# Nystromformer attention with a feed-forward layer: batch 0's turn and first products in parts, x blocks in pair tiles, and the order of steps written out as a list

## The chip, the cores and the metric

The kernel runs on one core of a Trainium2 chip. The metric is the device time of one execution in microseconds; the time of a kernel is the median of its runs. A core has a matrix engine (TensorE, PE in the profile; PEld is its loading of weights), VectorE (DVE), ScalarE (ACT), GpSimd (POOL), and DMA queues, issued here by SyncE (SP). Each engine takes its own instructions in the order in which the program gives them, and engines wait for each other through semaphores.

## The reference

Inputs are q, k and v of [8 batches, 8 heads, 576 rows, 64], float32, gains g of 512, and two weight matrices, W1 of 512 x 2048 and W2 of 2048 x 512. For each batch and head:

```python
q_lm = q.reshape(B, H, 32, 18, D).mean(axis=3)     # 32 landmarks
k_lm = k.reshape(B, H, 32, 18, D).mean(axis=3)
A, Bm, C = sm(q, k_lm), sm(q_lm, k_lm), sm(q_lm, k)  # softmax(a b^T / 8)
Z = Bm.T / (norm1(Bm) * norminf(Bm) + 1e-06)
for _ in range(6):
    Z = 2 * Z - Z @ Bm @ Z
attn = A @ Z @ C @ v
x = attn as [8, 576, 512]                            # heads side by side
xn = (x - mean(x)) / sqrt(var(x) + 1e-06) * g
out = x + maximum(xn @ W1, 0) @ W2
```

## The kernel before, in words

**Tiling.** Products are in float16 with float32 sums in PSUM. Two heads share a tile (a "unit"); a batch has four of them (two tiles of four heads for the wide stages). The landmarks are sums over groups of 18 rows, made on PE (`sums`, batch 0) or on DVE. The softmaxes have no division where it can be put off: `ea` is exp of the scores of q against the key landmarks (A), `ec` that of k (C), and `st` holds Bm's product and the iterate side by side, so that one iteration (`iterate`, line 817) is eight small matmuls and one DVE instruction (2 st - psum). `gram_of` (797) makes the start of the iteration: a matmul with `bones` adds the columns, another makes the gram matrix; then DVE takes the maximum, a reciprocal and a product.

**Fewer steps than the reference.** C v, then Z of that, give `cv` and `zt`. The attention's rows x are needed only for the norm's statistics and the last sum; the first layer takes the product of A with `zt` W1 (`m16`, made by `First.products`, line 1440, from `w` and `zt`), and so works from ea (`psh <- ea, m`, four matmuls of 288 columns for each of the 16 chunks of 2048). W1 is scaled by the gains when it comes (`scale_w1`, 478, on POOL or ACT) and centred. For batch 0, which starts before W1's column means are known, a correction ("lesser", `less_mean`, 1393) stands in for it: four matmuls of 512 columns for each quarter of W1. The second layer runs 512 columns at a time over 16 chunks, from batch 4 on with some products of sums (`mix_ahead`, `seven_products`).

**Stages and order.** Batches run in sets (1), (2), (3,4), (5,6), (7) behind batch 0. Batch 0's attention is `attention0` (610): its order is written out, with yields between which the launch sequence (1916) puts loads and scalings. Before it, `turn_tile` (571) transposes each of four q and k tiles, nine blocks each, into `pst`, whose copy to `xT` ACT makes; the last tile's copy is one DVE copy of 1152 columns. `warm` (552) puts matmuls on a tile of zeros where PE would wait.

Everything later is given by five generators: attention, totals of landmarks, first layers, first rows, second layers. `run` (1888) asks at each turn a clock model (`Clock`, 85) which of them could go now and takes the first of them; `help_out` (1761) issues loads, casts, DVE jobs, statistics (`measure`), centring, and mixing between them, by when an engine is modelled to be free, and a table `AFTER` (1830) holds some steps back until others have been taken. The generated program is fixed before it runs; on the chip only the order within each engine and the semaphores are left.

**Rows.** For batches 5, 6 and 7 two blocks of 128 rows of x are made together (`two_rows`, 857): their products stand in PSUM by head parity, and four copies of 256 columns bring them into two tiles `xblk` of a pool of twelve (`xpool`), all four on the engine that is modelled to be free sooner (`sooner`, 604). All other blocks are made whole or in parts (`rows_of`, `part_of_rows`). `finish_block` takes the statistics, `second_layer` adds the product to the block in place, and `store` (1375) sends it out, after which its tile is free.

All instructions but matmuls (line 318), transposes on PE (322) and loads are issued through `keep`, so the profile puts them all on line 312. The W1 loads are line 475, the stores 1380.

Of the kernel before, what the change touches and what calls it, by code (L numbers as in the profile page):

```python
# [9 lines left out]
FP16 = mybir.dt.float16  # L10
# [10 lines left out]
def kernel(  # L21
# [26 lines left out]
    D2 = 2 * (D + 1)  # L48
# [24 lines left out]
    def keys_of(ap):  # L73
# [3 lines left out]
        at = [ap.offset]  # L77
# [7 lines left out]
    class Clock:  # L85
# [46 lines left out]
        def took(self, i, e, n, m):  # L132
# [3 lines left out]
            if e == "Pool":  # L136
# [4 lines left out]
                return 100 + 0.92 * n if "Copy" in op else 280 + 1.76 * n  # L141
            if n == 1152 and "Copy" in op:
                return 760
# [18 lines left out]
        def note(self, i):  # L162
# [26 lines left out]
            if type(i).__name__ == "InstDMACopy":  # L189
# [7 lines left out]
                late_ = 1500 if self.issued <= 5 else 600 + min(2200, 0.8 * (self.wire - start - 1650))  # L197
                done = self.wire + late_
                start = done
            elif e == "PE":  # L200
# [19 lines left out]
                else:  # L220
# [10 lines left out]
                    self.free[e] = start + (8 if rows_ == 64 and cols < 128 else 4)  # L231
# [15 lines left out]
            for n in reads:  # L247
                self.used[n] = max(self.used.get(n, (0.0, e)), (done, e))
                if n.startswith("m16") and ":" in n:
                    self.begun[n[:n.index(":")] + "."] = done  # L250
# [125 lines left out]
    zeros = const.tile([P, 256], FP16, name="zeros")  # L376
# [84 lines left out]
    xpool = Ring(name="xpool", bufs=12)  # L461
# [10 lines left out]
    def load_w1(i):  # L472
        f, half = divmod(i, 2)
        stg = stage.tile([P, 2, DM], FP32, name="wstg", tag="stg")
        keep(nc.sync.dma_start(out=stg[:], in_=w1_src[:, 2 * half:2 * half + 2, ts(f, DM)]))
# [81 lines left out]
    x_blk = {}  # L557
# [6 lines left out]
    nat_pss, early_xT = {}, {}  # L564
# [6 lines left out]
    def turn_tile(w, nm):  # L571
# [6 lines left out]
        last = (w, i) == (U - 1, 1)  # L578
        pst = ps2.tile([P, NJ, P], FP16, name="pst", tag="p2")
        if last:  # L580
            sums(w, i, n16)
        for j in range(NJ):
            TR(pst[:, j, :], n16[:, j, :, :].rearrange("p r d -> p (r d)"), ident16[:])
        if not last:
            scalar.copy(t[:], pst[:])
            sums(w, i, n16)
        return t, pst

    def divisors(ea):
# [5 lines left out]
        act(lns[:], lns[:], AF.Exp, scale=-1.0)  # L595
        return lns[:].rearrange("p a t -> p (a t)")

    def normalize(ea, engine):
        engine.tensor_tensor(out=ea, in0=ea, in1=divisors(ea), op=ALU.mult)
# [10 lines left out]
    def attention0():  # L610
# [18 lines left out]
        banks.release(*banks.held)  # L629
        dve.tensor_copy(out=last_tile[0][:], in_=last_tile[1][:])  # L630
        yield "landmarks"
# [8 lines left out]
        st, bmT = softmax_of(psb, W)  # L640
# [1343 lines left out]
```

## Time and profile before

| what | before |
|---|---|
| median of three runs | 263.51 us (263.14 to 263.57) |
| profiled execution, span | 261.4 us |
| around the span (median less span) | 2.1 us |
| PE busy | 252.8 us, 3519 matmuls |
| DVE, ACT, POOL busy | 209.9, 171.8, 136.8 us |
| DMA | 46.68 MB, 179 GB/s on the mean |

The profile is of one execution. "Busy" is the time in which an engine ran an instruction; idle time of an engine other than the bound costs nothing by itself. In the rows of the time line a line gives start, length, engine, source line, operation, output and inputs, and count; in brackets stands the idle time before it and the engine and tile that ended it. Matmuls overlap, so of two rows the difference of their starts is read, and not the length.

### The profile page before, as it was taken

The page shows a single profiled execution, that of the slowest core. Times are in us where ns is not written, and L with a number is a line of the kernel's source. Part 1 is how long each engine was busy: PE and PEld are TensorE (multiplying, and loading weights), DVE is VectorE, ACT ScalarE, POOL GpSimd, SP SyncE. Part 2 cuts the span into 40 slices and gives each one's busy share as a digit, 9 for nine tenths or more (in the row PEclk, how much of TensorE's full clock was granted, in tenths as well). Part 3 has the DMA queues.
Part 4 walks back from the last instruction along what each step waited for, and adds up shares of the span by engine and source line. Part 5 has one row for each costly group of instructions (what it writes and reads, how often), then busy time and mean ns, then how long its engine had stood idle before and what let it go on. Part 6 is the DMA issues. An engine that isn't in the chain of part 4 may idle for free.

```text
span 261.4 us, 8559 instructions
## 1 busy us (share of the span) xinstructions
PE 252.8 (97%) x3519; PEld 167.7 (64%) x3519; DVE 209.9 (80%) x480; ACT 171.8 (66%) x332; POOL 136.8 (52%) x162
## 2 busy tenths in 40 slices
PE   7899999999999999999999999999999999999994
PEld 6645754556455574546655466588878875888883
DVE  2767965999979997899996972999399889696862
ACT  2588986458956878489986669634977863766000
POOL 5288779999951889899899955400000014000000
PEclk9999999999999999999999999999999999999999
DMA  6999999999947998669731101110330007100705
GB/s 238 381 393 381 384 391 387 355 251 345 349 145 213 282 375 308 185 158 336 244 84 43 26 21 40 45 38 3 80 84 4 3 11 162 32 3 0 163 19 182
DMA packets 24142, 46.68 MB, mean 179 GB/s; under 512 B 2980, under 2 KB 3240, under 8 KB 24104
## 3 DMA queue, kind: packets, MB, share of 16 engines
q1 hardware_dynamic: 23624, 45.50, 54.5%
q10 hardware_dynamic: 480, 0.66, 0.7%
q8 instruction: 27, 0.44, 0.7%
q14 instruction: 11, 0.09, 0.1%
HBM read 36.70 MB, written 9.44 MB: 177 GB/s over the span
## 4 chain that ended last, share of the span: by engine, by line
PE 82%; DVE 11%; DMA 3%; ACT 2%; issue 1%; SPq 0%; DVEq 0%
PE bank L318 53%; PE psh L318 21%; DMA stg<-in_q_dram 3%; DVE m L312 2%; PE psd L318 2%; PE pscv L318 2%; DVE six L312 1%; DVE xblk L312 1%; DVE w L312 1%; DVE part L312 1%; ACT hT L312 1%; PE psea L318 1%; DVE nat L312 1%; DVE xT L312 1%; PE psec L318 1%
## 5 line engine op out<-in xcount | busy, mean ns | idle before, releaser
L318 PE MATMUL bank<-w,hT 128*128 128x512 f16 (+3 forms) x528 | 109.5, 335 | 0.0
L312 ACT ACTIVATE hT<-psh 128x576 f16<-128x576 f32 x123 | 76.7, 655 | 23.9 <-PE psh L318 22.2
L318 PE MATMUL psh<-ea,m 128*128 128x288 f16 x512 | 79.0, 286 | 0.4 <-DVE ea L312 0.3
L318 PEld LDWEIGHTS <-hT 128*128 128x128 f16 x656 | 60.3, 98 | 29.5 <-issue 4.7
L318 PEld LDWEIGHTS <-m 128*128 128x128 f16 x512 | 49.4, 98 | 19.3 <-issue 2.8
L312 DVE SCALAR_TENSOR_TENSOR xblk<-bank,rstd,xblk 128x256 f32<-128x256 f32 (+2 forms) x77 | 39.2, 543 | 14.8 <-PE bank L318 14.6
L312 POOL TENSOR_TENSOR ea<-ea,lns 128x576 f16<-128x576 f16 x14 | 18.2, 1318 | 53.1 <-ACT lns L312 51.8
L312 POOL CAST nat<-stg 128x1152 f16<-128x1152 f32 x23 | 26.1, 1147 | 11.3 <-DVE xT L312 8.7
L312 DVE BATCH_NORM_STATS2 six<-xblk 128x6 f32<-128x512 f32 x36 | 24.3, 674 | 0.6 <-ACT xblk L312 0.5
L312 POOL CAST natv<-stg 128x1152 f16<-128x1152 f32 (+1 forms) x17 | 19.4, 1166 | 9.4 <-DMA stg<-in_v_dram 7.9
L312 DVE STREAM_TRANSPOSE xT<-nat 128x576 uint32<-128x576 uint32 x28 | 21.2, 759 | 0.0
L318 PE MATMUL bank<-w2mix,hT 128*128 128x256 f16 x128 | 17.7, 273 | 0.0
L318 PE MATMUL bank<-w2mix 128*128 128x256 f16 x128 | 17.4, 273 | 0.0
L312 DVE SCALAR_TENSOR_TENSOR st<-st,bank 128x128 f16<-128x128 f16 (+3 forms) x36 | 13.2, 366 | 5.0 <-PE bank L318 4.8
L312 ACT ACTIVATE lns<-psd 128x576 f32<-128x576 f32 x16 | 10.3, 645 | 7.9 <-PE psd L318 7.7
L312 DVE TENSOR_REDUCE part<-xT 128x32 f16<-128x576 f16 x20 | 14.3, 744 | 0.1
L312 ACT COPY xblk<-bank 128x512 f32<-128x512 f32 (+1 forms) x19 | 11.0, 592 | 4.9 <-PE bank L318 4.8
L312 POOL TENSOR_TENSOR asum<-asum 128x256 f32<-128x256 f32 (+1 forms) x20 | 13.0, 650 | 1.6
L318 PEld LDWEIGHTS <-w2mix 128*128 128x128 f16 x128 | 12.3, 98 | 2.0
L312 ACT ACTIVATE ec<-psec 128x256 f16<-128x256 f32 (+1 forms) x42 | 12.0, 430 | 1.9 <-PE psec L318 1.8
L318 PEld LDWEIGHTS <-st 32*32 32x32 f16 (+1 forms) x380 | 6.5, 90 | 10.5 <-DVE st L312 6.3
L312 POOL TENSOR_TENSOR asum<-nat 128x512 f32<-128x512 f16 x10 | 11.7, 1172 | 1.1 <-ACT nat L312 0.4
(133 smaller groups left out, 375.2 us busy)
## 6 DMA issues: line engine op xcount, KB each, us to landing
stg<-in_q_dram SPq DMA_DIRECT2D x16, 576.0 KB, 6.7
stg<-in_k_dram SPq DMA_DIRECT2D x15, 576.0 KB, 6.0
out_dram<-xblk SPq DMA_DIRECT2D x66, 128.0 KB, 2.4
wstg<-in_moe_w_ch_dram SPq DMA_DIRECT2D x16, 512.0 KB, 7.2
stg<-in_v_dram SPq DMA_DIRECT2D x5, 576.0 KB, 7.7
stg<-in_v_dram SPq DMA_DIRECT2D x40, 72.0 KB, 2.8
stg<-in_v_dram SPq DMA_DIRECT2D x6, 288.0 KB, 5.7
stg<-in_v_dram SPq DMA_DIRECT2D x12, 144.0 KB, 3.1
```

The source lines that it names most:

```text
L312: return lambda *args, **kw: keep(getattr(self.engine, op)(*args, **kw))
L318: keep(nc.tensor.matmul(o, l, r, start=start, stop=stop, tile_position=(rb, cb), skip_group_check=(skip or cb != 0)))
```

## The change

Instructions of all kinds stay what they compute; the parts are:

1. **Pair tiles.** `x_of` gives two neighbouring blocks one tile [128, 2, 512] from a pool of 5; the last block of an uneven batch (block 4 of each nine) has a tile of its own from a pool of 2. `two_rows` makes 2 copies of 512 columns in place of 4 of 256, and each goes to the engine that is modelled to be free sooner: 6 on DVE and 6 on ACT, where there had been 20 and 4.
2. **Batch 0's last turn.** The last k tile is cast in two halves as before, with another pattern; of its nine transposes six stand ahead of the landmark products and three behind the first q scores; four go to `pst` and five to a bank, and two DVE copies (512, 640 columns) replace one of 1152.
3. **Batch 0's order.** Scores and iterations are interleaved otherwise: landmark product, q scores of the first tile, the three transposes, k scores, q scores of the second tile, then the gram, in a bank of its own and with no filler in between; the k scores of the second tile stand behind the first iteration; the turn of the gains (`scaled_by_pe`) stands behind the gram. `ea` of the first tile is scaled whole by POOL, that of the second in halves by DVE as before. The copies to `zt` go from ACT to DVE. The first products `m16` are copied in parts of 128, 128 and 256 columns (before 256, 256). The correction of W1's second quarter stands behind the first two chunks of the first layer and not ahead of them, those of the third and fourth a chunk later.
4. **W1's first quarter** is loaded by four DMAs of 256 KB, before two of 512 KB. POOL scales four pieces of it, then `ea`, then nine more.
5. **The filler** at the start is 11 matmuls of 384 columns and three times two of 384, before 27 of 160, three times three of 256, and six in the gram and products: 25 matmuls fewer.
6. **The list.** `help_out`, `AFTER` and the choice by the clock model are gone; `ORDER` names 12 kinds of step and is issued as it stands. A step that cannot be issued yet is kept and tried again after each following one. Stores and the norm's deviations are still issued by the clock model (`settle`).

On the engines: PE 3494 matmuls (3519), DVE 468 instructions (482), ACT 340 (340), POOL 170 (167). Two changes of the shape of PE tiles fewer (131, before 133).

The core of the diff:

```diff
-    xpool = Ring(name="xpool", bufs=12)
+    xpool = Ring(name="xpool", bufs=5)
...
-            x_blk[j] = xpool.pin(xpool.tile([P, DM], FP32, name="xblk", tag="xblk"))
+            if j % 9 == 4:
+                t = xpool.pin(xpool.tile([P, 1, DM], FP32, name="xblk", tag="xone", bufs=2))
+            else:
+                t = xpool.pin(xpool.tile([P, 2, DM], FP32, name="xblk", tag="xblk"))
...
-            copy = sooner(1024, clock.at(t))
-            for i, (j, _) in enumerate(mine):
-                for hp in range(2):
-                    copy(crossed(x_of(j), hp), to[:, hp, i, :, :].rearrange("p u (r d) -> p u r d", r=2))
+            for hp in range(2):
+                sooner(512, clock.at(t))(
+                    crossed(x, hp), to[:, hp, :, :, :].rearrange("p i u (r d) -> p i u r d", r=2))
...
-            for r in (range(2) if (nm, u) == ("k", U - 1) else (slice(0, 2),)):
-                dve.tensor_copy(out=t[:, :, r, :] if isinstance(r, int) else t[:].rearrange("p j r d -> p r j d"),
-                                in_=raw[nm, u][:, r, :, :])
+            for r in range(2) if (nm, u) == ("k", U - 1) else (None,):
+                if r is None:
+                    dve.tensor_copy(out=t[:].rearrange("p j r d -> p r j d"), in_=raw[nm, u][:])
+                else:
+                    dve.tensor_copy(out=t[:, :, r, :].rearrange("p j (a d) -> p a j d", a=2),
+                                    in_=raw[nm, u][:, r, :, :].rearrange("p j (a d) -> p a j d", a=2))
...
+        if f == 0:
+            parted[stg.name] = DM
+            for c in range(2):
+                keep(nc.sync.dma_start(out=stg[:, c, :], in_=w1_src[:, 2 * half + c, ts(f, DM)]))
...
+        turn(range(NBEFORE))
+        last_turn.extend((t, pst, rest, turn))
...
-        dve.tensor_copy(out=last_tile[0][:], in_=last_tile[1][:])
-        yield "landmarks"
+        t, pst, rest, turn = last_turn
+        dve.tensor_copy(out=t[:, 0:NFIRST, :], in_=pst[:, 0:NFIRST, :])
...
-        for w in range(W):
-            scores_of_q(w)
+        scores_of_q(0)
+        turn(range(NBEFORE, NJ))
+        scores_of_k(0)
+        scores_of_q(1)
+        st, bmT = softmax_of(psb, W)
+        dve.tensor_copy(out=t[:, NFIRST:NJ, :], in_=rest)
+        banks.release(*last_bank)
+        lns = []
+        _, csum = gram_of(p1([P, 4, W * LM], "psse"), st, bmT, W, None, p1([P, 4, W * LM], "gram"))
+        lns.append(divisors(ea[0], 0))
+        scaled_by_pe()
...
-            scalar.copy(zt[:, :, w, :], pszt[:, :, 0:LM])
-        copy_mean(0)
-        scale_w1(3, 1, scalar)
...
+        normalize_by(pool, ea[0], lns[0])
...
+        for w in range(W):
+            dve.tensor_copy(out=zt[:, :, w, :], in_=pszt[w][:, :, 0:LM])
...
-        less_mean(1)
         next(a0)
...
-            if m in (2, 5):
-                f = 2 if m == 2 else 3
+            if m in (1, 3, 6):
+                f = (m + 3) // 3
...
+    ORDER = (
+        "2 3 4 215 3 23 M 2 J2 3 22 J3 2 1 3 2 M 22 L J 0 J 2 J 12 L 2 1 2 42 3 M 0 4 0 L 3 2 "
...
+        for k in order + [None] * 400:
+            settle()
+            late = [x for x in late if not issue(x)]
...
+            elif k in late or not issue(k):
+                late.append(k)
...
-    warm(27, 160)
+    warm(11, 384)
...
-            warm(3, 256)
+            warm(2, 384)
```

In `ORDER` a digit or letter is a kind of step and the number behind it how many of them: 0 attention, 1 totals, 2 first layers, 3 first rows, 4 second layers, J a DVE job of the batches to come, M statistics, C centring of W1, X and W mixing, K a cast, L a load.

More of the change, by code (lines that the diff above doesn't have):

```diff
@@ L47 @@
     UP = 16.0
-    D2 = 2 * (D + 1)
+    D1, D2 = D + 1, 2 * (D + 1)
     scale_qk = 1.0 / (D ** 0.5)
@@ L1929 @@
         load_w1(i)
+        if i < 2:
+            for c in range(2):
+                scale_w1(i, c, pool)
+    for it in range(7):
+        next(a0)
+    for i in range(2, 8):
         for c in range(2):
-            if i % 2 == 0 or c == 0 or i == 1:
+            if i % 2 == 0 or c == 0:
                 scale_w1(i, c, pool)
@@ L1948 @@
             b1.next_cast(part={"V": None, "A": 0, "B": 1}[what])
-    for it in range(6):
-        next(a0)
-    next(a0)
     run()
-    help_out(True)
+    settle(True)
 _INS = ['q', 'k', 'v', 'moe_g_ln', 'moe_w_ch1', 'moe_w_ch2']
```

375 lines of the change are left out of this document (191 added, 184 removed), and 30 rows, old and new, of tables (AFTER, ORDER).

## The prediction

> **What bounds the kernel now.** I read the page first: busy time by engine, the slices, the chain that ended last.
>
> ```profile
> span 261.4 us, 8559 instructions
> ...
> PE 252.8 (97%) x3519; PEld 167.7 (64%) x3519; DVE 209.9 (80%) x480; ACT 171.8 (66%) x332; POOL 136.8 (52%) x162
> ...
> PE   7899999999999999999999999999999999999994
> ...
> GB/s 238 381 393 381 384 391 387 355 251 345 349 145 213 282 375 308 185 158 336 244 84 43 26 21 40 45 38 3 80 84 4 3 11 162 32 3 0 163 19 182
> ...
> PE 82%; DVE 11%; DMA 3%; ACT 2%; issue 1%; SPq 0%; DVEq 0%
> ```
>
> The matrix engine is the bound: 97% busy, 82% of the last chain. So only two things can shorten the run: matmul time that is removed, and time in which PE waits. The DMA works at some 385 GB/s in slices 2 to 7 (6.5 us each), so what is wanted early cannot simply come earlier. The table of windows says where PE is not full:
>
> ```profile
> 0.00:22.00 22.00, 18.03 (x319) 12.43 (x320) 13.21 (x41) 11.88 (x18) 13.15 (x38) 1.00 0.94 342
> 22.00:66.00 44.00, 43.40 (x514) 25.52 (x511) 36.95 (x84) 33.12 (x66) 39.07 (x41) 1.00 1.02 354
> ```
>
> Columns: window, its sum, then busy us and count of PE, PEld, DVE, ACT, POOL, the clock, the DMA share, GB/s. In the first 22 us 3.97 us of PE are empty, and part of its 18.03 is filler on zeros; in the next 44 only 0.6. The two places to price are therefore the start (batch 0's chain through DVE and ACT) and a few short stalls behind it. The span is 261.4 us, the median of the runs 263.51, so 2.1 us lie around the span; I add the change to the median.
>
> **The change part by part.**
>
> *Batch 0's chain.* PE, DVE and ACT rows of the start (start, length, engine, operation, count, idle before):
>
> ```profile
> 10.71 0.44 PE L318 MATMUL bank<-pm,nat 128*128 128x64 f16 x9 [0.21 <-DVE nat L312]
> 10.98 0.67 PE L322 MATMUL pst<-ident,nat 128*128 128x128 f16 x9
> ...
> 11.73 0.22 PE L318 MATMUL bank<-lm 64*32 64x32 f16 x8
> ...
> 13.15 0.19 PE L318 MATMUL bank<-st,bones 128*128 128x64 f16 x1
> ...
> 13.67 0.93 PE L318 MATMUL psa<-xT,lm 64*32 64x512 f16 x16
> 14.54 0.24 PE L318 MATMUL bank<-st 32*32 32x64 f16 x8
> ```
>
> ```profile
> 11.18 0.29 DVE L312 CAST lm<-bank 128x128 f16<-128x128 f32 x1 [0.20 <-PE bank L318]
> 11.68 0.76 DVE L312 COPY xT<-pst 128x1152 f16<-128x1152 f16 x1 [0.21 <-PE pst L322]
> 12.43 0.22 DVE L312 TENSOR_REDUCE rsum<-bank 128x2 f32<-128x64 f32 x1
> ```
>
> ```profile
> 12.94 1.19 ACT L312 ACTIVATE ect<-psc 128x576 f16<-128x576 f32 x2 [0.72 <-PE psc L318]
> ```
>
> ```profile
> L312 DVE CAST nat<-stg 128x1152 f16<-128x1152 f32 x3 | 2.3, 760 | 5.2 <-DMA stg<-in_q_dram 4.5 <-DMA stg<-in_k_dram 0.7
> L312 DVE CAST nat<-stg 128x576 f16<-128x576 f32 x2 | 1.5, 754 | 0.0
> ```
>
> Cast: PE waits at 10.71 for the second half of the last k. A half costs 754 ns, a whole tile of twice the elements 760. The change gives the halves another pattern. Bounds: 380 ns (half of 760) to 754 (no change); I take 450, nearer the whole tile's rate. Gain 0.30, sums from about 10.41. [...]
>
> Transposes: six instead of nine (some 0.07 each) and no gains' turn stand before the products at 11.73. They then wait for the landmarks' cast (11.18, 0.29), with the cast's gain at about 10.88 to 11.17, so they start near 11.22, 0.5 earlier. The three transposes left follow on PE behind the first q scores, where PE waits anyway. The row sum at 12.43 was behind the 0.76 copy; the copy of 512 columns is at most 0.38 by the same row's rate, and the sum follows ACT at about 11.76. Next late is ACT: the second q scores stand ahead of the bones matmul and need the buffer that the first exponential frees, 0.6 long (ACT's two of 1.19) and starting at about 11.75 behind that of the products (11.22, 0.22 on PE, and an estimated 0.3 for the small exponential, as the casts and sums of 64 or 128 columns take 0.22 to 0.29); bones goes from 13.15 to about 12.8. From there the gram had stood behind filler in one bank with the column sum; the gap from 13.15 to the first iteration's 14.54 shrinks from 1.39 to about 1.05, and the 0.93 us of q scores no longer lie in it. First iteration about 13.85, 0.7 earlier. The six iterations are a chain from PE to DVE and back, whose instructions the change leaves as they are, so their step stays.
>
> The rest of the chain:
>
> ```profile
> 19.07 0.52 PE L318 MATMUL bank<-w,zt 64*32 64x512 f16 x8 [0.25 <-ACT zt L312]
> 19.67 1.18 PE L318 MATMUL bank<-w,lesser 128*128 128x512 f16 x4
> 20.69 0.41 PE L318 MATMUL psh<-ea,m 128*128 128x288 f16 x2
> 21.38 1.14 PE L318 MATMUL psh<-ea,m 128*128 128x288 f16 x6 [0.28 <-DVE ea L312]
> ```
>
> ```profile
> L312 DVE TENSOR_TENSOR ea<-ea,lns x4: 444/450/818, 18.3 to 21.2; 128x288 f16<-128x288 f16 x4
> ```
>
> ```profile
> L312 POOL TENSOR_TENSOR ea<-ea,lns 128x576 f16<-128x576 f16 x14 | 18.2, 1318 | 53.1 <-ACT lns L312 51.8 <-PE pszc L318 1.3
> ```
>
> ```profile
> 16.25 6.60 POOL L312 TENSOR_SCALAR w<-wstg,g_sb 128x512 f16<-128x512 f32 x8 [0.28 <-DMA wstg<-in_moe_w_ch_dram]
> ```
>
> Behind the iterations the first products with W1 come about 0.6 earlier (18.45; DVE, which now makes both copies of zt in front of them, is assumed to lose 0.1 on ACT). Then PE ran 4 matmuls of the second quarter's correction ("lesser"), started the first chunk and waited 0.28 on DVE, which has four halves of ea to scale (shortest, median and longest in the tile's row). Two of them go to POOL as one instruction; the second chunk, of which the 21.38 group holds four (its start 21.87 by 122 ns a matmul), can start at about 20.62, 1.25 earlier. But the four lesser matmuls (4 x 0.216 = 0.86) that had lain in this wait now come behind the two chunks, on PE's full stretch. Net **-0.4**. Bounds: +0.4 (ea late, the 0.86 paid, 0.46 gained) and -1.0.
>
> POOL's ea must be in time: 1.32 us on POOL (the form's mean in later batches) between the scalings of W1 at 0.825 us each. It postpones the nine scalings behind it by 1.3 us; the second quarter is wanted only with the correction that now comes later, so I price that at nothing; if that cover goes, it costs up to 1.3. W1's four loads of 256 KB move the same bytes through SP's queue, two issues more; nothing, as the wire is the limit (385 GB/s), and the first half of a quarter can only land earlier.
>
> *Stalls of the body.* Where PE waits behind 22 us, and what the written list puts there:
>
> ```profile
> 34.46 1.00 PE L318 MATMUL psec<-xT,lm 32*32 32x288 f16 x32
> 35.73 0.19 PE L318 MATMUL bank<-st,bones 128*128 128x64 f16 x1 [0.27 <-DVE st L312]
> ...
> 40.74 0.24 PE L318 MATMUL bank<-st 32*32 32x64 f16 x8 [0.25 <-DVE st L312]
> ...
> 66.25 0.67 PE L318 MATMUL psec<-xT,lm 32*32 32x288 f16 x28
> 66.86 2.55 PE L318 MATMUL bank<-w,hT 128*128 128x512 f16 x11
> 69.24 0.19 PE L318 MATMUL bank<-st,bones 128*128 128x64 f16 x1
> 69.61 0.28 PE L318 MATMUL bank<-st 128*128 128x128 f16 x2 [0.17 <-DVE st L312]
> ...
> 76.20 0.59 PE L318 MATMUL bank<-w,hT 128*128 128x512 f16 x2
> 76.94 0.31 PE L318 MATMUL bank<-st 128*128 128x160 f16 x2 [0.15 <-DVE st L312]
> ```
>
> ```profile
> 39.60 0.69 DVE L312 BATCH_NORM_STATS2 six<-xblk 128x6 f32<-128x512 f32 x1 [0.53 <-ACT xblk L312]
> 40.43 0.25 DVE L312 SCALAR_TENSOR_TENSOR st<-st,bank 128x128 f16<-128x128 f16 x1
> ```
>
> A matmul of 512 columns takes 0.216 (66.86 to 69.24 for 11). Batch 1: psec to bones lasted 1.27, where 28 of the 32 took 0.61 at 66.25; about 0.6 is empty, and two matmuls of 512 (0.43) are put there: -0.4. Its first step at 40.74: the 0.69 of statistics stood ahead of the step's DVE instruction at 40.43; the list puts them behind: -0.3. Batch 2: bones ends at about 69.27, the next starts at 69.61 on DVE's st; 13 instead of 11 matmuls stand between: -0.34. Its step before 76.94: 0.74 for two matmuls of 0.216, 0.31 empty; the spacing is made more even: -0.2. Together -1.25. The list is issued without regard to the time, so elsewhere it can make new ones: I allow +0.4. Body: **-0.85**.
>
> *Tile form.* Two changes of form fewer on PE (131 against 133 by the order of both kernels).
>
> ```profile
> 44.22 0.60 PE L318 MATMUL bank<-w,hT 128*128 128x512 f16 x2
> ...
> 44.91 0.60 PE L318 MATMUL bank<-w,hT 128*128 128x512 f16 x2
> ```
>
> From 44.22 to 44.91 are 0.69, of which 0.43 are two matmuls: into small tiles and out costs 0.26 with the small matmuls between. Bounds 0 to 0.26; **-0.2**.
>
> *Pair tiles.* For batches 5 to 7:
>
> ```profile
> L312 DVE COPY xblk<-psr 128x256 f32<-128x256 f32 x20 | 7.1, 417 | 0.0
> ```
>
> Four copies of 256 columns (20 on DVE, 4 on ACT in all) become two of 512, six on each. One of 512 costs between one and two of 256, 0.42 to 0.83, so DVE loses 3.3 to 5.8 us of its 8.3 and ACT gains at most 3.3. Both engines have room and PE does not wait here, so **0**. If the cover goes: a pair holds two blocks until both are stored, and a wait for a pair tile delays one group of row matmuls, a few tenths.
>
> Sum: -0.4 - 0.85 - 0.2 = -1.45; 263.51 - 1.45 = **262.1 us**.
>
> **The rivals.**
> *R1, the start's gain is swallowed.* Batch 1's attention waits for its loads (the wire is full to 52 us), so an earlier start only shifts the wait. For it: slices 2 to 7. Against: PE has first-layer work of batch 0 to fill with. Also the case that the halved cast does not get faster. -1.05: 262.5.
> *R2, slower: the written list has no time check.* A DVE instruction of 0.69 ahead of an iteration's st step (as at 39.60) costs PE up to that. There are some 30 such steps. They take the place of the 0.4 allowed, so 1.85 of gains stand against them: three hits (2.07) are the point from which it is slower at all, four give 2.76 - 1.85 = +0.9, 264.4, five 265.1. For it: nothing holds a step back any more. Against: the places that I followed in the new order are spaced as the old ones or better.
> *R3, DVE slowed by POOL.* With ea on POOL, DVE's remaining halves run beside it. One of the four took 0.82 instead of 0.45, so both may: +0.74, -0.71 in all, 262.8. Against: POOL was busy from 16.25 without a break, and only one of four halves was slow. [...]
> *R4, more.* The correction's matmuls fall into other waits (a full -1.25) and no new stall appears: -1.25 - 1.25 - 0.2 = -2.7, 260.8.
>
> **How the numbers follow.** Forecast 0.40, R1 0.12, R3 0.08, R4 0.10, all faster than 263.51 by over 0.2% (0.53 us, about what a measurement of this kernel can tell from no change). R2 with two or three hits (263.0 to 263.7), within it: 0.12. R2 with more: 0.18. So 0.70, 0.12, 0.18. The range reaches from 260.2 (R4, with 0.6 more by the start's bound of -1.0) to 264.6 (R2 with four hits); it leaves out R2 with five or more, 0.1, and as little below.
>
> **What would show it.** In the changed kernel: the second half of the last k cast at 0.45 and not 0.75; first iteration at about 13.85; first W1 products at 18.45; second chunk at about 20.6 with four lesser matmuls behind it; the gaps before 35.7, 40.7, 69.6 and 76.9 gone; DVE's copies of rows shorter by 3.3 us or more. It would be wrong if PE showed new waits of 0.3 or more on DVE's st in the iterations of batches 1 to 7, or if PE waited for ea past 21.

## The result, and the profile after

The changed kernel takes 264.95 us (median of 6 runs, 264.48 to 266.12), the kernel before 263.32 (6 runs, three of them those of the table above). The ratio is 1.0061, interval 1.0042 to 1.0081: **slower by 0.6%, where 0.55% faster had been forecast**. The profiled execution has a span of 262.8 us (before 261.4). Medians here and below are of all runs, and the ratios leave out the few runs that took over 1.5% more than the fastest of their kernel.

The page of the changed kernel, first the lines that answer to those of before:

```profile
span 262.8 us, 8511 instructions
...
PE 253.7 (97%) x3494; PEld 166.5 (63%) x3494; DVE 204.4 (78%) x466; ACT 174.0 (66%) x332; POOL 139.7 (53%) x165
...
PE   7879999999999999999999999999999999999994
...
PEclk9986999999999999999999999999999999999999
...
GB/s 250 353 398 385 386 387 361 368 231 296 359 208 202 159 324 356 175 180 190 374 192 41 23 42 42 42 40 2 36 128 2 4 3 159 42 2 0 159 23 180
...
PE 83%; ACT 5%; POOL 3%; DVE 3%; DMA 3%; issue 2%; SPq 0%; ACTq 0%; POOLq 0%; DVEq 0%
```

PE does 25 matmuls less and is busy 0.9 us longer. The line to see is PEclk, the clock that PE was granted: 8 and 6 in slices 3 and 4 now, where the page of before has

```profile
PEclk9999999999999999999999999999999999999999
```

In the table of windows of the changed kernel (columns as in the prediction; the one before the DMA's share is the clock) this is a step:

```profile
15.00:16.00 1.00, 0.95 (x34) 0.46 (x26) 0.55 (x2) 1.00 (x3) 1.00 (x2) 1.00 1.07 406
16.00:17.00 1.00, 0.57 (x23) 0.32 (x20) 0.30 (x2) 0.97 (x3) 1.00 (x3) 1.00 1.02 387
17.00:18.00 1.00, 0.18 (x9) 0.17 (x8) 0.00 (x0) 0.33 (x1) 1.00 (x1) 0.79 1.06 399
18.00:19.00 1.00, 1.00 (x19) 0.32 (x14) 0.62 (x4) 0.00 (x0) 1.00 (x3) 0.50 1.04 383
...
23.00:24.00 1.00, 1.00 (x6) 0.61 (x5) 1.00 (x4) 0.65 (x1) 0.82 (x2) 0.50 1.05 393
24.00:25.00 1.00, 1.00 (x5) 0.45 (x4) 0.65 (x2) 0.73 (x2) 1.00 (x3) 0.79 1.00 349
```

From 17.59 to 24.41 us PE runs at half its clock. Ahead of it PE stands still, and the time line of PE says on what:

```profile
16.07 0.24 PE L322 MATMUL bank<-st 32*32 32x64 f16 x8
16.24 0.37 PE L322 MATMUL pscv<-natv,ect 64*64 64x130 f16 x11
17.82 0.48 PE L322 MATMUL pscv<-natv,ect 64*64 64x130 f16 x9 [1.22 <-issue]
...
20.94 0.63 PE L322 MATMUL bank<-w,zt 64*32 64x512 f16 x8
22.11 2.12 PE L322 MATMUL psh<-ea,m 128*128 128x288 f16 x8 [0.54 <-DVE m L316]
24.03 1.23 PE L322 MATMUL bank<-w,lesser 128*128 128x512 f16 x4
```

The wait of 1.22 us lies in the middle of twenty matmuls with the same inputs, and "issue" means that PE waited for nothing that the profile shows. In the kernel before the same stretch has no wait:

```profile
15.83 0.24 PE L318 MATMUL bank<-st 32*32 32x64 f16 x8
15.99 0.49 PE L318 MATMUL bank<-natv,ect 64*64 64x130 f16 x20
```

The eight matmuls at 22.11 take 0.24 us each (to 24.03), twice the 0.122 of before (eight from 29.88 to 30.86).

Where the time goes is seen best when both kernels are read at the same amount of matmul work: columns times the form of a matmul over 128*128, the largest form in the rows, filler left out. As the orders of the two differ, a figure is good to about 0.2 us. Microseconds by which the changed kernel is behind the one before:

```
time in the kernel before  15.4   17.6   19.9   23.1   33.8   46.2   99.1   250
changed                   -0.4   +1.5   +2.6   +2.5   +2.9   +2.4   +1.6   +1.3
```

It is ahead at 15.4, loses 3.0 us between 15.4 and 20, and wins back 1.3 by the end.

### The profile page after: what moved, and what is told of

The parts are those of the page before. It is cut to its first block, busy times and chain, and to the rows that moved or that the text cites. A ratio compares the mean times of both kernels' runs of the same rounds, so it can differ in the third digit from the quotient of the medians.

```text
span 262.8 us, 8511 instructions
## 1 busy us (share of the span) xinstructions
PE 253.7 (97%) x3494; PEld 166.5 (63%) x3494; DVE 204.4 (78%) x466; ACT 174.0 (66%) x332; POOL 139.7 (53%) x165
## 4 chain that ended last, share of the span: by engine, by line
PE 83%; ACT 5%; POOL 3%; DVE 3%; DMA 3%; issue 2%; SPq 0%; ACTq 0%; POOLq 0%; DVEq 0%
PE bank L322 53%; PE psh L322 23%; DMA stg<-in_q_dram 3%; POOL asum L316 2%; PE pscv L322 2%; ACT hT L316 1%; PE psec L322 1%; POOL ea L316 1%; PE psea L322 1%; ACT xblk L316 1%; PE psd L322 1%; ACT m L316 1%; PE psr L322 1%; ACT ea L316 1%; DVE st L316 0%
## 5 line engine op out<-in xcount | busy, mean ns | idle before, releaser
L322 PE MATMUL bank<-w,hT 128*128 128x512 f16 (+3 forms) x528 | 111.1, 334 | 0.0
L316 ACT ACTIVATE hT<-psh 128x576 f16<-128x576 f32 x126 | 79.2, 654 | 19.1 <-PE psh L322 17.8
L322 PE MATMUL psh<-ea,m 128*128 128x288 f16 x512 | 80.6, 288 | 0.7 <-DVE m L316 0.5
L316 POOL TENSOR_TENSOR ea<-ea,lns 128x576 f16<-128x576 f16 x15 | 19.5, 1314 | 49.3 <-ACT lns L316 49.3
L316 POOL CAST nat<-stg 128x1152 f16<-128x1152 f32 x25 | 28.9, 1172 | 11.5 <-DVE xT L316 7.9
L316 POOL CAST natv<-stg 128x1152 f16<-128x1152 f32 (+1 forms) x17 | 19.3, 1163 | 12.5 <-DMA stg<-in_v_dram 8.7
L316 ACT CAST m<-bank 128x512 f16<-128x512 f32 x17 | 9.8, 591 | 6.0 <-PE bank L322 5.2
```

Source lines behind the costliest of these rows:

```text
L316: return lambda *args, **kw: keep(getattr(self.engine, op)(*args, **kw))
L322: keep(nc.tensor.matmul(o, l, r, start=start, stop=stop, tile_position=(rb, cb), skip_group_check=(skip or cb != 0)))
```

## The experiments

**Theory F**: PE's instructions reach it in blocks; the block that PE needs behind its 223rd matmul came late, the 1.2 us of wait are that, and with the idle time the clock falls. **Theory D**, its rival: the clock falls since less filler and a sparser chain leave PE too little work, with or without that wait. A third, **R1** of the prediction, has the loads of the start swallow any gain.

In each of these kernels all other instructions keep their order on every engine, but for what the edit says (and one filler matmul more in the mended ones below); without pair tiles the planner also gives some copies and some of hT's activations to the other of DVE and ACT. "Before" is always run beside it. The excerpts below leave out a third argument of `warm`, which keeps the planner's clock model at the old filler, and a wider tile of zeros where the kernel before needs one.

**1 and 2: filler given back in two ways.** At the start (same time, 19 matmuls more), or in the iterations (six more):

```diff
-    warm(11, 384)
+    warm(27, 160)
...
-            warm(2, 384)
+            warm(3, 256)
```
```diff
             st = iterate(p1, st, it, W)
+            warm(1, 256)
```

> The changed kernel with the start's filler of the kernel before: 27 matmuls of 160 columns and three times three of 256 in place of 11 and three times two of 384. PE's filler time stays as it is (4320 and 768 columns against 4224 and 768), 38 PE instructions more stand ahead of batch 0's chain, all else is in the same order. Theory F (PE's instructions come in blocks, and the block that PE reaches at its 224th matmul came too late: 1.2 us of wait with no releaser at 16.6 us, and this wait lets the granted clock fall to half from 17.6 to 24.4 us): the block's end lies at an earlier and slower part of the chain, so the wait is under 0.5 us, the clock stays at 1.00, and the time falls by 2 us or more, to 262 to 263. Theory D (the clock falls because less filler and a sparser chain leave too little matmul work in the stretch 14 to 17.6 us, with or without that wait): the clock still falls, 264.5 to 265.5.

> The changed kernel with one filler matmul of 256 columns behind each of batch 0's six iterations (0.65 us of matmul work more between 14.2 and 19.5 us, where PE waits for DVE). Theory D: the clock stays at 1.00 and the time falls by some 2 us, to 262 to 263, though the instruction wait may stay. Theory F: the wait stays (the block's end is reached at most 4 matmuls earlier in the chain), the clock still falls, 264.5 to 265.5.

Start: 263.18 us, ratio 0.999 (0.997 to 1.0011). The wait is 0.5 us at the same count of matmuls, the clock 0.997 or more in 8 of 10 runs. Iterations: 264.24, ratio 1.0044 (1.0014 to 1.0074), wait 1.6 us in the profile, clock under 0.997 in 5 of 10 (changed kernel: 0.978 to 0.987 in all six). The matmuls given back at the start take no more PE time than those they replace (5.2 us, there 5.4); that alone takes 1.8 us off. That is F. But filler in the iterations keeps the clock up in half of the runs though the wait of its profile is longer, so D holds a part: in these runs the clock fell with the wait and the thin stretch together.

**3 and 4: the filler taken from the kernel before**, at the start, and there and in the attention:

```diff
-    warm(27, 160)
+    warm(11, 384)
...
-            warm(3, 256)
+            warm(2, 384)
...
-        warm(4, 256)
+        warm(1, 64)
...
-        cinv, _ = gram_of(p1([P, 4, W * LM], "psse"), st, bmT, W, lambda: warm(2, 256))
+        cinv, _ = gram_of(p1([P, 4, W * LM], "psse"), st, bmT, W, lambda: warm(1, 64))
```

> The kernel before with the start's filler of the changed one (11 of 384, three times two of 384): 38 PE instructions fewer ahead of the chain, the same filler time. Theory F: the block's end moves 19 matmuls later in the chain, into iterations 3 and 4; a wait with no releaser of 0.3 to 1.2 us appears between 16 and 18 us, and with it a fall of the clock: 264.5 to 266.5. Theory D: nothing changes, 263.3 within 0.3, clock 1.00.

> The kernel before with the start's filler of the changed one and the six filler matmuls of 256 columns in the attention of batch 0 reduced to two of 64: 0.6 us less matmul work between 11.9 and 13.5 us, 46 PE instructions fewer. Theory F: as with the start's filler alone, a wait and a fall of the clock, 264.5 to 266.5. Theory D: the fall of the clock appears here and not with the start's filler alone, 265 to 266.5. If neither holds (the removed filler is without effect): 263.3 within 0.3.

263.77, ratio 1.0025 (1.0006 to 1.0044), and 264.24, ratio 1.0031 (1.0007 to 1.0056); the expected size was too large. The wait appears in both, at the same count of matmuls as in the changed kernel. PE rows of the kernel before with the start's filler alone changed:

```profile
16.09 0.42 PE L318 MATMUL bank<-natv,ect 64*64 64x130 f16 x15
17.30 0.27 PE L318 MATMUL bank<-natv,ect 64*64 64x130 f16 x5 [0.78 <-issue]
```

The clock fell in 3 and 4 of 10 runs. So a part of the change that computes nothing makes the kernel before slower by itself. The two profiles also price the wait and the clock apart. With both thinned PE waited 0.87 us and kept its full clock in that run: at the same work the kernel is 1.0 us behind at 17.6 and 0.8 at 99. With the start alone it waited 0.78 and ran at half clock for 6.83: it is 2.1 behind at 99. So here the wait cost about its own length, and the fall of the clock some 1.3 us more.

In the trace the transfers on the instruction queue can be followed (q8 of the page: 27 with 0.44 MB, before and after, so 16 KB each). To 3519 matmuls with their weight loads they are one for about 128. Behind 100 us, where the loads no longer fill the DMA (under 200 GB/s in 22 of the 25 slices there on the page of before), two in three begin within 1 us of the 95th matmul or of a 128th behind it (27 such places up to the 3423rd). So I take these for the places at which a block is asked for, and the one at matmul 95 for that of the block needed behind matmul 223; no trace shows the asking itself. Work resumed 1.2 to 1.5 us after the landing in each kernel with a wait (late: the landing and 1.3 us, less the time at which the block was needed):

```
                      95th matmul  transfer from-to   needed   late
before                   10.9       13.21-14.14       15.9     no (0.4 to spare)
changed                  11.6       15.48-16.53       16.4     1.4
filler at the start      10.6       13.97-14.95       15.6     0.7
filler in iterations     10.8       15.37-16.42       16.1     1.7
before, start thinned    11.9       15.02-16.07       16.3     1.1
```

The transfer starts 2.3 to 4.6 us behind the 95th matmul in this stretch, in which the loads fill the DMA (353 to 398 GB/s from 6.5 to 19.6 us, by the pages of before and of the changed kernel). The chain between is dense in small matmuls, 128 in 4.4 to 5.3 us. What delays a transfer no run shows; the waits that went with it were up to 1.6 us.

**5 to 8: the block ends moved.** 64 short filler matmuls in place of 17, so that the ends fall earlier in the chain; then the same with two repairs of the chain, without pair tiles, and in the kernel before:

```diff
-    warm(11, 384)
+    warm(33, 128)
...
-            warm(2, 384)
+            warm({('q', 0): 6, ('k', 0): 18, ('q', 1): 7}[nm, w], 128)
```
The two repairs (called "mended" below):
```diff
             if it == 5:
-                less_mean(0, 2, 3)
+                less_mean(0, 2, 4)
+                scale_ea(1, 0)
...
-        less_mean(0, 3, 4)
...
-        scale_ea(1, 0)
```

> The changed kernel with 64 short filler matmuls (33, 6, 18 and 7 of 128 columns) in place of 17 of 384: 47 matmuls more stand ahead of batch 0's chain, so that the ends of PE's instruction blocks (95th and 223rd matmul) fall at about 8.3 and 14.7 us. 18 of them fill 0.7 us of the idle time before the third tile's turn; no filler stands in the chain itself. Theory F: the second block is there in time (asked for at 8.3, it took 4.6 to 6.1 us until now), no wait without a releaser before 20 us, the clock stays at 1.00 in nearly all runs, median 262.0 to 262.6. Theory D (too little matmul work from 14 to 17.6 us): the clock still falls in many runs, median 263.2 or more, as with the start's filler of the kernel before (263.18).

> As the shifted one, and in batch 0 the last correction matmul of W1's first quarter stands ahead of the Z products and not behind them, and the first half of ea's second tile is scaled ahead of the copies to zt. If the changed kernel's first chunk waits for these two (its copy of the correction ends 0.6 us later than before beside the W1 products, and PE waits 0.5 to 0.7 us for m): the wait before the first chunk falls under 0.3 us and the time by 0.3 to 0.7 us against the shifted one. If it waits for the W1 products' own way through DVE: within 0.2 us of the shifted one.

> As the shifted one, without pair tiles: twelve tiles of one block, four copies of 256 columns by one engine for two blocks in batches 5 to 7. If the pair tiles give nothing on the path (as forecast): within 0.3 us of the shifted one. If the body's regained time comes from them: slower by 0.5 to 1.0 us. If they cost (a pair is held until both blocks are stored): faster by 0.3 or more.

> The kernel before with the same filler at the start (64 short matmuls in place of 36; 28 more instructions' pairs ahead of the chain), its six in the attention kept. Its own block end moves from 15.7 to about 14.6 us. It has no wait there in its profile, so: 263.1 to 263.5, no change, but fewer runs above 263.6, if those come from the late block. If the shift itself costs: 263.7 or more.

Shifted: 263.61, ratio 1.0011 (0.999 to 1.0031). The wait at 16 us is gone and the clock 0.998 or more in 11 of 12 runs, as F has it, but the time is 1 us above what it expected. Mended: 263.69, no difference. Without pair tiles: 264.47, ratio 1.0034 (1.0014 to 1.0055). Kernel before, shifted: 264.13, ratio 1.0025 (1.0003 to 1.0046), against the expectation of no change, with a clock of 0.997 or more in all runs; its profiled execution, 261.1 us of span, doesn't show why: it is among the shortest of twelve spans from 260.8 to 263.6.

The trace of the shifted kernel says where its gain went: it is 1.0 us ahead at 23 us, behind by 0.4 at 34, 0.8 ahead at 99, 0.2 ahead at 104 and 0.8 behind at 157. The waits of its PE:

```profile
PE psh L322 <- DVE m L316: 1.4, 3, 0.6
PE bank L322 <- issue: 0.6, 1, 0.6
PE psea L322 <- issue: 0.4, 1, 0.4
```

The two on "issue" are other blocks: the transfer of the one at 102 us began 3.8 us behind its place and landed 0.7 too late, 9 x 128 matmuls behind the first; the other is at 154 us, 16 x 128 behind it. Moving the ends cured one late block and made two.

**9 to 12: the loads of W1, and ea on DVE.** The first quarter of W1 in two DMAs again, in the changed kernel and in the shifted one; there also with ea's first tile scaled by DVE, and with the mended chain:

```diff
-        if f == 0:
...
+        keep(nc.sync.dma_start(out=stg[:], in_=w1_src[:, 2 * half:2 * half + 2, ts(f, DM)]))
```
```diff
             if it == 5:
                 less_mean(0, 2, 3)
+                scale_ea(0, 0)
...
-        normalize_by(pool, ea[0], lns[0])
...
+        between.append(lambda: scale_ea(0, 1))
```

> The changed kernel with W1's first quarter loaded by two DMAs of 512 KB, as before the change, all else in the same order. If the four DMAs of 256 KB make the hole in the loads (140 to 180 GB/s between 11.5 and 12.7 us in each kernel with them, 290 to 340 without): the hole is gone, W1's later pieces and batch 1's k land 0.4 us earlier. The block of PE instructions is then asked for at the same place, so theory F has the wait at the 224th matmul (0.6 to 1.2 us) and the fall of the clock stay: 264.2 to 265.0. If the hole is what makes the block late: no wait, clock 1.00, 262.5 to 263.3.

> The shifted kernel with the two DMAs of 512 KB. In the shifted one PE waits 1.1 us between 23.6 and 26.3 us for m, whose correction waits for W1's second and third quarter, which land 0.5 to 0.7 us later than in the kernel before. If the four small DMAs cause that: the later quarters land 0.4 to 0.7 us earlier, these waits shrink under 0.6 us, 262.9 to 263.3 (shifted: 263.61). If not: within 0.2 us of the shifted one.

> As the shifted kernel with the two DMAs of 512 KB, and ea's first tile is scaled by DVE in halves, as before the change, and not by POOL. If POOL's ea costs (1.28 us between the scalings of W1, and one DVE half of 0.68 to 0.89 beside POOL in place of 0.45): W1's second quarter is scaled 1.3 us earlier, and the time falls by 0.2 to 0.5 us against the same kernel with ea on POOL. If it gains, as forecast (DVE has two halves fewer ahead of the second chunk): slower by 0.3 to 0.8 us.

> The shifted kernel with the two DMAs of 512 KB, the correction's last matmul ahead of the Z products and the first half of ea's second tile ahead of the copies to zt. The candidate for the fastest: the wait for m before the first chunk under 0.4 us and the later waits under 0.6, 262.4 to 263.0 where no block of PE instructions is late in the body. If the later quarters of W1 set the pace anyway: within 0.2 us of the shifted one with two DMAs.

265.01 (ratio 1.0057, 1.0034 to 1.0079), 263.49 (1.0016, 0.999 to 1.0042), 263.43 (1.0006, 0.9976 to 1.0036), 263.77 (0.9995, 0.9965 to 1.0024). The hole in the loads goes with the four DMAs, as expected (from 11.6 to 12.5 us 142 GB/s in the changed kernel, some 310 in the first of these); W1's last piece came only 0.15 to 0.2 us earlier, and the time hardly changes. The late block stays without them (1.4 us, clock 0.979 to 0.987 in all 12 runs of the first), so the small DMAs don't cause it. ea on DVE or POOL can't be told apart by the times.

**13 and 14: all block ends where none should be late.** From the delays seen so far I chose 29 matmuls more than in the changed kernel:

```diff
-    warm(11, 384)
+    warm(25, 168)
...
-            warm(2, 384)
+            warm({('q', 0): 4, ('k', 0): 12, ('q', 1): 5}[nm, w], 192 if nm == 'k' or w == 0 else 160)
```

> The changed kernel with 46 filler matmuls at the start (25 of 168 columns, 4 and 12 of 192, 5 of 160) in place of 17: 29 matmuls more ahead of the chain. By the times at which the blocks of PE instructions landed in the runs so far (the next matmul 1.3 us after the landing; the transfer starts 2 to 4 us after the block before it was begun where the loads fill the DMA, 0 to 1.5 us elsewhere), no block end falls where it is late: not at 16 us, not at 102, not at 154. Theory F whole: no wait without a releaser over 0.2 us, clock 1.00, lag against the kernel before under 0 from 40 us on, 262.3 to 263.0. If a time of 263.4 or more comes without such waits and at clock 1.00, late blocks are not what keeps the changed kernel from its gain.

> The same with W1's first quarter in two DMAs of 512 KB, the correction's last matmul ahead of the Z products and the first half of ea's second tile ahead of the copies to zt. Without late blocks: 0.3 to 0.6 us under the kernel with the same filler, 261.9 to 262.6, below the kernel before.

**262.18 us, ratio 0.9947 (0.9923 to 0.9971)**, clock 0.998 or more in all 7 runs: here the change with 29 filler matmuls more is faster by what had been forecast (the kernel before took 263.87 on that chip, 263.2 to 263.6 on the others). With two W1 loads and the mended chain 263.48, ratio 0.9977 (0.9951 to 1.0003), clock under 0.997 in 7 of 12 runs: it waits 1.03 us ahead of the first W1 products, for DVE's copies to zt, and its clock falls behind that (in the profile at 20.4 us):

```profile
19.41 0.54 PE L322 MATMUL bank<-w,zt 64*32 64x512 f16 x8 [1.03 <-DVE zt L316]
```

PE of the first of the two:

```profile
13.76 0.24 PE L322 MATMUL bank<-st 32*32 32x64 f16 x8 [0.20 <-DVE st L316]
...
15.20 0.67 PE L322 MATMUL pscv<-natv,ect 64*64 64x130 f16 x16
15.80 0.24 PE L322 MATMUL bank<-st 32*32 32x64 f16 x8
15.96 0.49 PE L322 MATMUL pscv<-natv,ect 64*64 64x130 f16 x20
...
18.25 0.54 PE L322 MATMUL bank<-w,zt 64*32 64x512 f16 x8
19.38 1.70 PE L322 MATMUL psh<-ea,m 128*128 128x288 f16 x8 [0.59 <-DVE m L316]
20.91 1.03 PE L322 MATMUL bank<-w,lesser 128*128 128x512 f16 x4
...
24.67 1.03 PE L322 MATMUL psh<-ea,m 128*128 128x288 f16 x7 [0.32 <-DVE m L316]
```

**15 to 18: single parts on that base, and the same kernel once more**: the mended chain with four W1 loads, without pair tiles, ea on DVE, and no edit at all.

> The changed kernel with 29 matmuls more of start filler, and in batch 0 the correction's last matmul ahead of the Z products and the first half of ea's second tile ahead of the copies to zt; W1's first quarter in four DMAs. With the four DMAs the W1 products no longer wait for their weights (1.0 us with two DMAs), so the wait for m before the first chunk should fall from 0.6 to under 0.4: 261.8 to 262.1. If the later quarters of W1 set the pace from 23 us on: as without this edit, 262.2 within 0.3.

> The same filler without pair tiles (twelve tiles, four copies of 256 columns by one engine). The forecast's step (they give nothing on PE's path): 262.2 within 0.3. As the shifted kernels differ (264.47 without, 263.61 with): 262.7 to 263.1, with the time lost in batches 5 to 7, from 157 us on.

> The same filler with the first tile of ea scaled by DVE in halves and not by POOL, W1 in four DMAs. If moving ea to POOL gains at the second chunk, as the forecast has it: slower by 0.3 to 0.8 us, 262.5 to 263.0. If POOL's 1.28 us between the scalings of W1 takes back what DVE gains: 262.2 within 0.3, or faster.

> The changed kernel with 29 matmuls more of start filler once more, on another chip than its first run. Its first late block was at the edge there (landed 0.2 us late), and in the three kernels that each change one part of it, on another chip, 0.4 to 0.7 us late with the clock falling in many runs (263.4 to 264.0). If the gain of 0.5% is the kernel's: ratio 0.993 to 0.997. If it hangs on the edge, where a few tenths of lateness let the clock fall: ratio 0.998 to 1.001, with clocks of 0.993 in a third of the runs or more.

263.99 (ratio 1.0017, 0.9992 to 1.0041), 263.56 (1.001, 0.9984 to 1.0036), 263.36 (0.9996, 0.997 to 1.0022), and the same kernel again 263.17 (0.9988, 0.9968 to 1.0008). The block behind matmul 223 was 0.2 us late in the first profile and 0.4 to 0.7 in these four, all beginning their transfer 3.3 to 3.9 us behind the 95th matmul. So the two runs of one kernel, on two chips, differ by 1 us: a gain of 0.1 to 0.5%, at the edge of a late block; the second alone can't be told from no change. Their profiles, which hold the same matmuls, part at that place: 0.4 us at matmul 224, and 1.5 more by matmul 317, most of it while the second run is at half clock (16.17 to 19.58). Of the three parts only the pair tiles can be read, from the trace and not from the times (below).

## Why the prediction was wrong

**The step that failed** is the first one: "part of its 18.03 is filler on zeros", by which PE's time in the first 22 us was counted as empty, and no term of the sum stood for the 25 matmuls removed. But each of them, with its weight load, had set the ends of PE's instruction blocks one place earlier in the chain (the wait behind the 223rd matmul, 1.22 us here, came with 0.78 in the kernel before when the start's filler alone was changed). Measured: 3.0 us lost between 15.4 and 20 us, by the wait of 1.22 and by half clock from 17.59 on. That the removed filler had also held the clock up by its own work is not shown: with the six in the attention thinned too, the clock fell in 4 of 10 runs, without that in 3. No rival had it, and R2, the only one on the slow side, was wrong in its mechanism: behind 22 us no wait of the changed kernel's PE on DVE's st is longer than 0.2 us. Slower had 0.18.

That this cause is the one is shown by giving back filler alone (264.95 to 263.18, then 262.18 and 263.17), and by taking it from the kernel before (263.36 beside it, to 263.77 and 264.24).

**The clock's grid.** In the traces the granted clock kept a value for a multiple of 3.41 us, but at the end of the run. In the changed kernel it was full from 7.35 us on for 10.24, half for 6.83, full for 238.93; before, full from 6.03 on for 256.00; in the second run of the kernel with 29 filler matmuls more, half for 3.41 (16.17 to 19.58). So I cut each run into windows of 3.41 us from a change of its clock. Their starts differ from run to run (the grids of the two profiles of the kernel with 29 filler matmuls lie 1.4 us apart), which I take for the reason that one kernel runs with and without the fall. What sets the falls apart in these traces is the matmul work in such a window. Take columns times the form's share of 128*128, over what 3.41 us hold at 0.216 us for 512 columns, in the nineteen profiles at full clock:

```
windows at full clock            work in the window
clock at half behind it      9   0.25 to 0.31
clock still full          1371   0.33 and more
```

The two don't overlap, while by PE's busy time they do (0.54 to 0.83 where it fell; as little as 0.59 where it didn't). Wherever behind 5 us a window starts, the kernel before has none under 0.36; the changed one comes down to 0.27 before its clock falls. So the late block is why PE waited, and I take the window made thin by the wait, in a chain of small matmuls (0.27 in the changed kernel), for why the clock fell: a wait of 0.87 whose window held 0.36 left it up. No window lies between 0.31 and 0.33.

**Batch 0's chain** (-0.4). Right in part. The half cast took 0.46 us (0.45 was an estimate between half of 0.76 and the 0.754 of before; what in the new pattern makes it faster no run shows):

```profile
10.16 0.46 DVE L316 CAST nat<-stg 128x576 f16<-128x576 f32 x1 [0.29 <-DMA stg<-in_k_dram]
```

It began 0.3 later than in the profile of before, since that k landed at 10.14 and not at 9.87. With the blocks in time the first iteration begins at 13.76 (forecast 13.85) and the W1 products at 18.25 (18.45). Part of that is luck, as the last k landed at 9.57 in that run: from its landing to the first iteration are 4.67 us before, 4.03 in the changed kernel and 4.19 here, so 0.5 to 0.6 were gained and not 0.7. The first chunk then starts at 19.38, where 0.59 are lost on m: the list of what is late next was short of the correction's copy, which ACT makes only behind a matmul that the change put behind the Z products (to 18.95; DVE, too, is on a half of ea until 18.94). Behind two chunks and the correction's four matmuls it is 0.67 ahead, where 0.4 had been forecast:

```profile
22.45 0.49 PE L318 MATMUL bank<-w,zt 64*32 64x512 f16 x8
```
```profile
21.78 0.65 PE L322 MATMUL psh<-ea,m 128*128 128x288 f16 x4
```

It falls back to +0.1 at 34, as PE waits for m, whose correction ACT copies behind a scaling that waited for W1's load (21.98, 0.21 ended by the DMA). So loads do swallow the start's gain, as in R1, but W1's and not batch 1's. (R4's -1.25 for this chain went beyond the bound of -1.0 that the prediction gave it.)

**Body** (-0.85, and -0.2 for tile forms, which no run shows apart). Right in sum: from 33.8 to 99.1 us the kernel with 29 filler matmuls goes from 0.1 behind to 1.1 ahead, and the changed one from 2.9 to 1.6. Of the four gaps, the one in batch 2 shows it best, 13 matmuls between psec and bones and no wait behind (before 69.24 to 69.61; here the kernel with 29 filler matmuls):

```profile
66.35 2.98 PE L322 MATMUL bank<-w,hT 128*128 128x512 f16 x13
69.16 0.19 PE L322 MATMUL bank<-st,bones 128*128 128x64 f16 x1
69.19 0.28 PE L322 MATMUL bank<-st 128*128 128x128 f16 x2
```

That this kernel ends 1.3 us ahead in its first profile, near the 1.45 of the sum, is partly luck: the chain had given nothing by 34 us, and 0.2 came behind 99, where no term stood.

**Pair tiles** (0). Wrong, on the good side. Two copies of 680 ns (DVE) or 586 ns (ACT) take the place of four of 417 (DVE's in all fall from 8.3 to 4.1 us, as forecast), and the DVE instruction on which PE waits behind them comes sooner. The DVE of the kernel with 29 filler matmuls, without and with pair tiles:

```profile
169.11 1.40 DVE L316 COPY xblk<-psr 128x256 f32<-128x256 f32 x4
170.44 1.28 DVE L316 TENSOR_TENSOR hT<-hT 128x1024 f16<-128x1024 f16 x2
171.64 0.86 DVE L316 SCALAR_TENSOR_TENSOR xblk<-bank,rstd,xblk 128x256 f32<-128x256 f32 x2
```
```profile
168.76 0.68 DVE L316 COPY xblk<-psr 128x512 f32<-128x512 f32 x1
169.36 1.28 DVE L316 TENSOR_TENSOR hT<-hT 128x1024 f16<-128x1024 f16 x2
170.56 0.86 DVE L316 SCALAR_TENSOR_TENSOR xblk<-bank,rstd,xblk 128x256 f32<-128x256 f32 x2
```

Without them PE waits for it,

```profile
172.56 0.49 PE L322 MATMUL bank<-w2mix 128*128 128x256 f16 x3 [0.21 <-DVE xblk L316]
```

and once more at 197.6. At these two places the same matmul starts 0.37 and 0.33 us later than with pairs, and at no other between 164 and 199: the kernel loses 0.7 us there; in the shifted kernels the medians differ by 0.86 us. "PE does not wait here" was read from the kernel before, whose order held other work at that place; the written list relies on the shorter copies.

**POOL beside DVE** (R3). Right in kind, and it hangs on the moment. The mended chain with two W1 loads, DVE and POOL:

```profile
17.81 1.41 DVE L316 TENSOR_TENSOR ea<-ea,lns 128x288 f16<-128x288 f16 x1
19.14 0.34 DVE L316 CAST zt<-pszt 128x64 f16<-128x64 f32 x2
```
```profile
17.62 1.28 POOL L316 TENSOR_TENSOR ea<-ea,lns 128x576 f16<-128x576 f16 x1
```

DVE's half takes 1.41 us in place of 0.45: it ends 0.32 us behind the end of POOL's instruction (18.90). So it does in the shifted kernel (DVE 18.16 to 18.84, POOL's ea to 18.52) and with 29 filler matmuls without pair tiles (18.48 to 19.19, POOL to 18.88). Where DVE began first (17.35, POOL 17.49, in the shifted and mended kernel), POOL's took 1.48. The mended chain put the half into POOL's ea and lost at zt what it had won at m. In the changed kernel one half of two took 0.86, but beside a scaling of W1 (DVE to 21.77, POOL to 21.46), like the slow one of four in the kernel before (to 21.33, POOL to 21.02). So POOL's scalings slow a half as its ea does, and the slow halves are not due to the move of ea alone, as R3 has it. In all these slow halves DVE ends 0.31 or 0.32 us behind POOL's instruction; what holds it no trace shows. The price was 0 to 1 us for a half, where I had 0.37 each: it went with what was left of POOL's instruction (1.09 us where the half took 1.41, 0.36 where it took 0.68).

What stays open: why the kernel before got slower when shifted, and why the same block's transfer starts 0.4 us later behind its place in one run of the kernel with 29 filler matmuls than in the other. Neither was tried.

## What to carry to other kernels

Filler matmuls are instructions, and may be what a kernel stands on (without 25 of them 3.0 us were lost here between 15.4 and 20 us): before counting their time as free, look at the granted clock and the matmul work in the stretches around them and at where the instruction blocks end (every 128 matmuls with their weight loads here). A wait with no releaser in the middle of a group, behind the 223rd matmul in five kernels (0.8 to 1.6 us), was a late block here; it was cured by moving the count, and each such move shifted the later blocks too (64 short filler matmuls: late ones at 102 and 154 us).

## What the runs showed of the hardware that I had not expected

- A block of PE instructions took about 1 us to move (13.21 to 14.14 before, 15.48 to 16.53 in the changed kernel) and, where PE waited for it, was used 1.2 to 1.5 us after landing. At the start, with loads at 373 to 385 GB/s from 8 to 20 us, its transfer began 2.3 to 4.6 us behind the 95th matmul.
- DVE's halves of ea, 0.45 us by themselves, took 0.68 to 1.41 us in the five cases above, beside POOL's ea or one of its scalings of W1, and ended 0.31 or 0.32 us behind the end of that.
- The clock was at half behind each window of the 3.41 us grid that had run at full clock with 0.31 of the possible matmul work or less, and behind none with 0.33 or more, in nineteen profiles. Behind one wait of 1.2 us among small matmuls it was at half for 6.8 us; behind the 0.94 us for which PE was idle from 8.3 on in the kernel before it stayed full, in a window that held 0.6.
- Four loads of 256 KB in place of two of 512 KB left a hole in the loads: from 11.6 to 12.5 us 140 to 200 GB/s on the mean in each of five kernels with four, 280 to 340 in seven with two.
